# Spectral filter and token mixer, two layers: normalised rows of the inverse steps one step later in ScalarE's order, the doubled tile's low part inside those steps, and the last rows of the first layer written in four pieces

## Chip, cores and metric

One core of a Trainium2 chip runs the whole kernel. The metric is the device time of one execution in microseconds. The kernel before took 1017.25 us as the median of 3 runs (1016.85 to 1018.95).

## What is computed

x is 2048 tokens by 640 channels, f32. A layer has two halves: a spectral filter over the layer-normalised x (2-D FFT, a product with complex weights, inverse FFT), and a token mixer, an MLP over the tokens. Each is added to x. Two layers follow each other with the same weights.

```python
def _A_ref(x, w_r, w_i):
    X = jnp.fft.rfft2(x, axes=(-2, -1))
    X = X * (w_r + 1j * w_i)
    return jnp.fft.irfft2(X, s=(S, D), axes=(-2, -1))

def _B_ref(x, w1, b1, w2, b2):
    h = _layernorm(x, axis=-1)
    u = jnp.einsum("bsd,sf->bdf", h, w1) + b1      # w1: 2048 x 1728
    u = _gelu(u)
    y = jnp.einsum("bdf,fs->bds", u, w2) + b2      # w2: 1728 x 2048
    return y.transpose(0, 2, 1)

x = x + _A_ref(_layernorm(x), A_w_r, A_w_i)
x = x + _B_ref(_layernorm(x), B_w1, B_b1, B_w2, B_b2)
x = x + _A_ref(_layernorm(x), A_w_r, A_w_i)
x = x + _B_ref(_layernorm(x), B_w1, B_b1, B_w2, B_b2)
```

## The kernel before

x lies in 16 row tiles of 128 tokens by 640 channels, numbered 0 to 15 (`NJ` = 16). Products that need more than half precision are made from pairs of f16 tiles: a high part (`...h`) and a low part (`...l`), the difference from the f32 value. A full product is three matmuls (high by high, low by high, high by low).

**Stages.** The first layer runs: the filter's forward stages (to about 130 us of the profile), its inverse steps (method `a2`, to about 184 us), the mixer's first product with W1 (`b1st`, to about 376 us), its second product with W2, row by row (still `b1st`, to about 562 us), and a tail that joins it to the filter's first stage of the second layer. The second layer has the same inverse steps (about 640 to 693 us) and a mixer of its own form (`b2nd`, to the end). 

**Inverse steps** (`a2`). Step i of NJ + 5 works on several rows at once, each in another phase: on row i the matmuls of one inverse stage and ScalarE's `eh`; on row i-1 VectorE's `el` and the matmuls of the other inverse stage; on row i-2 the additions to `xt` on VectorE and GpSimd, and the store; on row i-3 the layer norm's statistics on VectorE (`st`, `mv`, `v`); on row i-4 the scale `r` and offset `nb` on GpSimd (`r` by a power), and then `hf`, the normalised row, on ScalarE, for some rows with a f16 copy (`hha`, `hh`). The tiles `xt` have five buffers, and the load of row i+1 is issued in step i. The steps run in program order on every engine (`self.pin`, which makes the helper at line 59 keep each instruction's place), so an instruction that waits holds all that stands behind it on its engine. All compute instructions carry line 59, the helper's; they are told apart by their tiles.

**The doubled tile.** One weight tile of W1 has 64 columns left; its other half holds the low part of the same columns. `wsplit` writes it in two chunks: ScalarE the high columns into `wh` and a copy into `wl` (steps 12 and 13 of `a2`), VectorE the rest, `wh<-raw,s,wl`, two instructions of 128x512, at the start of `b1st` and of `b2nd`. In `b1st` the 16 subtractions `hl = hf - hh` follow on VectorE.

**Rows of the second product** (`b1st`). For each row j, 28 groups (14 tiles of the hidden width, two halves of 320 channels) of three matmuls, two for the short tile: 82. Then VectorE adds the PSUM tile to `xt` (`xt<-ps,c,xt`), which frees it, and the row is prepared for the next layer's filter: statistics (VectorE), `r` and `nb` (GpSimd), `z` (ScalarE), `eo` (first fold, GpSimd), `f` (second fold, VectorE), `fh` (ScalarE), `fl` (VectorE). s1, the filter's first stage, is 15 small matmuls `tM,fh`/`tM,fl` into a PSUM tile, and `s1h` (ScalarE) and `s1l` (VectorE) take it over. `pend` holds rows that wait for s1; `flush(k)` issues s1 until k rows are left. After row j `flush(1)` issues s1(j-2). The next rows' weight tiles are made on the way: `wh` on ScalarE, `wl` on VectorE. Until row 15 no order is pinned here and the scheduler sorts. Row 15 runs its two halves one after the other, in program order; between them, `flush(0)` issues s1(13), and the second fold and `fh` of row 14 are written. After the second half, `a0_tail` makes `fl` and s1 of row 14 and, in two parts (`ft`, `fht`, `flt`), all of row 15. The next stage (`tD,s1h`, `tD,s1l`) needs all 16 rows.

Of the kernel before, what the change touches and what calls it, by code (L numbers as in the profile page):

```python
# [10 lines left out]
F32 = mybir.dt.float32  # L11
# [3 lines left out]
AF = mybir.ActivationFunctionType  # L15
# [4 lines left out]
S, D, NL, F = 2048, 640, 321, 1728  # L20
NJ, NG, NFT = 16, 16, 14
# [13 lines left out]
HA = range(8)  # L35
# [31 lines left out]
class Layers:  # L67
# [644 lines left out]
    def a2(self, li):  # L712
        nc, A = self.nc, self.A
        first = li == 0
        V, G, T = self.V, self.G, self.T
# [9 lines left out]
        p = self.push("a2", side=self.sq)  # L725

        xts = [p.tile([128, 642], F32, name=f"xt{i}_{self.n}") for i in range(5)]
# [10 lines left out]
        def xload(j):  # L738
            nc.sync.dma_start(xts[j % 5][:, :D], self.xs[li][j])
            return xts[j % 5]  # L740
# [36 lines left out]
        xt, pd, eo, p1, ec, mv, vs, rb = ({} for _ in range(8))  # L777
# [3 lines left out]
        for i in range(NJ + 5):  # L781
            has = [0 <= i - k < NJ for k in range(6)]
            if has[0]:
                pd[i] = id_mm(i)
            if has[1]:
                k = i - 1
                eh, ps = eo[k], pd.pop(k)
                el = elow(ps, eh)
                if not first and i == NJ:
                    self.pss0 = self.big()  # L790
                    for j in HA:
                        for a in range(2):
                            mm(self.pss0[:, a, :320], self.w[0][0][:, j], self.hh[j][:, a], start=j == 0, stop=False)
                p1[k] = is1_mm(eo.pop(k), el, tIM[k // 4][:, k % 4])
            if first and i == 10:
                next(sc)
            if has[4]:
                v, mean = vs.pop(i - 4)
                r = self.t(p, [128, 1], F32, "r", 2)
                G.tensor_tensor(r, v, self.mh, op=ALU.pow)  # L800
                b = self.t(p, [128, 1], F32, "nb", 2)
                G.tensor_scalar(b, mean, r, -1.0, op0=ALU.mult, op1=ALU.mult)
                rb[i - 4] = r, b
            if has[2]:
                k = i - 2
                x, ps = xt[k], p1.pop(k)
                o = ps[:, 1]
                e = self.t(p, [128, 324], F32, "ec", 2)
                T.activation(e[:, :322], ps[:, 0, :322], AF.Copy)
                V.tensor_tensor(v2(x, 160, NL), v2(x, 160, NL), v2(o, 161, 1), op=ALU.subtract)  # L810
                V.tensor_tensor(x[:, :NL], x[:, :NL], o[:, :NL], op=ALU.add)
                if first and i == 11:
                    next(sc)
                G.tensor_tensor(v2(x, 160, NL), v2(x, 160, NL), v2(e, 161, 1), op=ALU.add)
                G.tensor_tensor(x[:, :NL], x[:, :NL], e[:, :NL], op=ALU.add)
            if has[4]:
                r, b = rb.pop(i - 4)
                f = self.hf[i - 4]
                T.activation(f, xt.pop(i - 4)[:, :D].rearrange("p (a b) -> p a b", a=2), AF.Identity, scale=r, bias=b)
                if i - 4 in HA:  # L820
                    T.activation(self.hh[i - 4], f, AF.Copy)
            if 1 <= i and i + 1 < NJ:
                xt[i + 1] = xload(i + 1)
            if has[2]:
                nc.sync.dma_start(self.xs[li + 1][i - 2], xt[i - 2][:, :D])
            if has[3]:
                st = self.stats1(p, xt[i - 3])
                m = self.stats2(p, st)
                v = self.t(p, [128, 1], F32, "v", 2)
                V.tensor_scalar(v, m[:, 1:2], (1.0 + EPS) / ZS ** 2, EPS * EPS / ZS ** 2, op0=ALU.mult, op1=ALU.add)  # L830
                vs[i - 3] = v, m[:, 0:1]
            if has[0]:
                eo[i] = ehigh(pd[i])
            if i == 3:
                self.wload(1)
                self.wopen(1)
            if first:
                if i in (6, 7):
                    self.scan1(1, (i - 6,))
                if i == 8:  # L840
                    sc = self.scale1(1, at=lambda: p1[i - 1][:, 1, 400:401])
                    next(sc)
            if i in (12, 13):
                self.wsplit(1, (i - 12,), lo=False)
            if i in (1, 4, 8):
                mload()
        self.pin = False
# [81 lines left out]
    def b1st(self, li):  # L929
        nc, A = self.nc, self.A  # L930
        V, G, T = self.V, self.G, self.T
# [5 lines left out]
                T.activation(self.hh[j], self.hf[j], AF.Copy)  # L937
        sc = {m: self.scale1(m) for m in range(2, NFT + NJ)}
        self.pin = True
        self.wsplit(1, hi=False)  # L940
        self.wload(2)
        self.scan1(2)
        self.h = []
# [13 lines left out]
        p = self.pz = self.push("b1", side=self.sq)  # L957
# [50 lines left out]
        for ft in range(NFT):  # L1008
# [10 lines left out]
            for j in run:  # L1019
# [20 lines left out]
                else:  # L1040
# [16 lines left out]
                    if ft >= NFT - 2 and 1 < j < 14 and j % 2 != ft % 2:  # L1057
                        i = SEQ[(j - 2) // 2 + 6 * (ft - NFT + 2)]
                        usplit(i, uf[i])
            dup, i = ft == 1, SEQ[ft]  # L1060
# [26 lines left out]
        p = self.pT  # L1087
# [10 lines left out]
        xts = [load(0), load(1)]  # L1098
        pend = []

        def flush(k):
            while len(pend) > k:
                self.s1_all(*pend.pop(0))

        for j in range(NJ):
            wh, wl = self.w.pop(NFT + j)
            ahead(NFT + j, (wh, wl))
            m = NFT + j
            steps = prep(m)
            c2 = self.ct[1][:, j:j + 1]  # L1110
            if j + 2 < NJ:
                xts.append(load(j + 2))
            xt = xts[j][:, :D]
            T.activation(xt, xt, AF.Identity, bias=self.b2[:, j:j + 1])
            x2 = xt.rearrange("p (a b) -> p a b", a=2)
            tail = j == NJ - 1
            ps = self.big()
            pss = (ps[:, 0], self.big()[:, 0] if tail else ps[:, 1])
            order = [(ft, a) for ft in SEQ for a in range(2)]
            if tail:  # L1120

                order.sort(key=lambda q: q[1])
                st = self.t(p, [128, 2, 6], F32, "st", 2)
                self.pin = True

            def half(a):
                V.scalar_tensor_tensor(x2[:, a], pss[a][:, :320], c2, x2[:, a], op0=ALU.mult, op1=ALU.add)
                V.bn_stats(st[:, a], x2[:, a])

            for i, (ft, a) in enumerate(order):  # L1130
                if tail and i == NFT:
                    half(0)
                    flush(0)
                    pend.append((j - 1, *self.a0_hi(self.a0_fold2(late))))
                if i in (4, 8):
                    next(steps, None)
                if i in (6, 7):
                    step(m + 2)
                if i in (15, 18):
                    self.scan1(m + 3, (i // 3 - 5,))  # L1140
                if i == 26 and m + 3 < NFT + NJ:
                    step(m + 3)
                o = pss[a][:, :320]
                if ft < NFT - 1:
                    self.mm3(o, (wh[:, ft], wl[:, ft]), (uh[ft][:, a], ul[ft][:, a]), ft == SEQ[0], ft == SEQ[-1])
                else:
                    mm(o, wh[:, ft], ul[ft][:, a], start=False, stop=False)
                    mm(o, wl[:, ft], uh[ft][:, a], start=False, stop=False)
            if tail:
                half(1)  # L1150
                nc.sync.dma_start(self.xs[li + 1][j], xt)
                self.a0_tail(j, xts[j], st, pend)
                self.pin = False
                break
            V.scalar_tensor_tensor(x2, ps[:, :, :320], c2, x2, op0=ALU.mult, op1=ALU.add)
            nc.sync.dma_start(self.xs[li + 1][j], xt)
            flush(1)
            r, b = self.stats_r(p, *self.stats(p, xt, self.CA, self.CB))
            late = self.a0_fold1(self.a0_norm(xt, r, b))
            if j < NJ - 2:  # L1160
                pend.append((j, *self.a0_lo(*self.a0_hi(self.a0_fold2(late)))))
        self.pop("a0")
        self.pop("u")
        self.pop("wr2")
# [14 lines left out]
    def b2nd(self, li):  # L1179
# [6 lines left out]
        V, T, G = self.V, self.T, self.G  # L1186
# [220 lines left out]
        first, last = (collections.defaultdict(list) for _ in range(2))  # L1407
        lam = lambda f, *a: lambda: f(*a)
        A2, A4 = slice(0, 2), slice(2, 4)
        for d in range(ND):  # L1410
            i = {a: at[d, a] for a in PB}
# [17 lines left out]
        self.pin = True  # L1429
        fetch(0)  # L1430
        fetch(1)
        self.wsplit(1, hi=False)
        pr = self.push("br", side=self.sp)
        (wh0, wl0), (wh1, _) = self.w.pop(0), self.w.pop(1)
        pss = self.pss0, self.big()
        early, late, low, high = range(NJ - 4), range(NJ - 4, NJ), range(8), range(8, NJ)
# [23 lines left out]
        p = self.push("b1", side=self.sq)  # L1460
# [94 lines left out]
        def xload(d):  # L1555
            if d < NQ:
                xts[d] = self.t(p, [128, 2, 2, 320], F32, "xt", 3)
                for i in range(2):
                    nc.sync.dma_start(row(d, i), self.xs[li][E[d] + NQ * i])
# [402 lines left out]
```

## Time and profile before

| | us |
|---|---|
| median of 3 runs | 1017.25 (1016.85 to 1018.95) |
| profiled execution | 1017.07 |
| its span, first to last instruction | 1015.3 |
| mean granted TensorE clock | 0.979 of full |

| engine | busy us |
|---|---|
| TensorE (PE) | 969.4 |
| VectorE (DVE) | 781.8 |
| ScalarE (ACT) | 576.5 |
| GpSimd (POOL) | 300.0 |

A row of a timeline gives the start, the time that the merged instructions cover (us), the engine, the line, the operation, the tiles (out<-in) with their shapes, how many instructions are merged, and in brackets the idle time of the engine before them with what ended it. Buffer numbers are left out, so `xt` is any row. Busy times of neighbours overlap a little, as each instruction's own latency is counted in; an engine's pace is read from the starts. In a row of waits stand the waiting engine and tile, the releaser, the total in us, how many waits, and the longest. In the table by stretches each engine has its busy time and, in brackets, its instructions; the three last numbers are the granted clock, the DMA engines' busy share and GB/s.

### The profile page before, as it was taken

How to read it: one execution, taken by the hardware profiler on the slowest of the kernel's cores; microseconds unless marked ns; L12 is line 12 of the kernel's file. 1: busy time of each engine (PE TensorE's matmuls, PEld its weight loads, DVE VectorE, ACT ScalarE, POOL GpSimd, SP SyncE). 2: the span in 40 equal slices, each digit the busy share in tenths (PEclk: the TensorE clock that was granted, in tenths of full speed). 3: DMA queues.
4: the chain of work that ended last, by engine and by line, in shares of the span. 5: the costliest groups of instructions: out<-in, count | busy, mean ns of one | idle time of the engine just before them, and what ended most of it. 6: DMA issues, size and time to landing. Idle time of an engine off the chain costs nothing.

```text
span 1015.3 us, 20992 instructions
## 1 busy us (share of the span) xinstructions
PE 969.4 (95%) x8235; PEld 721.2 (71%) x8235; DVE 781.8 (77%) x1493; ACT 576.5 (57%) x890; POOL 300.0 (30%) x502
## 2 busy tenths in 40 slices
PE   4889999999999999999999799999999999999998
PEld 3778777677777667777777688776777777677776
DVE  7978978988777784666666689789965557998885
ACT  5857668687666455555553377685643454544531
POOL 6937857412212201222222277574000000000000
PEclk9599999999999999999999999999999999999999
DMA  7865356557657546464423455365444446755411
GB/s 232 279 185 164 115 178 219 206 187 255 236 195 250 186 124 246 139 193 146 126 89 117 126 181 181 105 229 204 159 156 164 145 142 228 245 177 190 153 45 53
DMA packets 67259, 176.45 MB, mean 174 GB/s; under 512 B 7996, under 2 KB 15320, under 8 KB 67160
## 3 DMA queue, kind: packets, MB, share of 16 engines
q1 hardware_dynamic: 59384, 146.92, 45.1%
q0 software_dynamic: 7776, 28.20, 7.5%
q8 instruction: 64, 1.05, 0.4%
q14 instruction: 35, 0.29, 0.1%
HBM read 127.24 MB, written 47.84 MB: 172 GB/s over the span
## 4 chain that ended last, share of the span: by engine, by line
PE 36%; DVE 13%; ACT 6%; POOL 3%; issue 3%; DMA 2%; SPq 0%; ACTq 0%; DVEq 0%; POOLq 0%
PE ps L59 36%; DVE wl L59 3%; DMA xt<-x 2%; DVE st L59 2%; DVE xt L59 1%; POOL eo L59 1%; DVE f L59 1%; ACT wh L59 1%; ACT xt L59 1%; ACT z L59 1%; DVE s1l L59 1%; ACT junk L59 1%; POOL xt L59 1%; DVE Yl L59 1%; DVE S L59 1%
## 5 line engine op out<-in xcount | busy, mean ns | idle before, releaser
L59 PEld LDWEIGHTS <-wh 128*128 128x128 f16 x2602 | 251.9, 98 | 103.6 <-issue 5.0
L59 PEld LDWEIGHTS <-wl 128*128 128x128 f16 x1610 | 157.5, 98 | 66.0 <-DVE wl L59 2.8
L59 PE MATMUL ps<-ul,wh 128*128 128x320 f16 x448 | 133.9, 301 | 0.6 <-DVE ul L59 0.6
L59 PE MATMUL ps<-uh,wl 128*128 128x320 f16 x448 | 133.9, 301 | 0.1
L59 PE MATMUL ps<-uh,wh 128*128 128x320 f16 x416 | 124.8, 300 | 1.6 <-DVE s L59 1.6
L59 PE MATMUL ps<-hl,wh 128*128 128x320 f16 x496 | 102.2, 299 | 0.9 <-DVE hl L59 0.9
L59 PEld LDWEIGHTS <-wo 128*128 128x128 f16 x756 | 73.9, 98 | 29.4 <-DVE wo L59 0.8
L59 DVE SCALAR_TENSOR_TENSOR wl<-raw,s,wh 128x896 f16<-128x896 f32 (+2 forms) x64 | 75.0, 1176 | 12.9 <-ACT wh L59 12.7
L59 ACT ACTIVATE junk<-raw 128x896 bf16<-128x896 f32 (+1 forms) x60 | 59.5, 991 | 44.2 <-DMA raw<-w 44.0
L59 POOL TENSOR_TENSOR r<-v,mh 128x1 f32<-128x1 f32 x64 | 36.4, 569 | 158.4 <-DVE nm L59 149.0
L59 PE MATMUL ps<-tDi,Yh 128*128 128x322 f16 x320 | 71.3, 300 | 0.2
L59 DVE TENSOR_TENSOR f<-eo 128x256 f32<-128x256 f32 (+1 forms) x124 | 39.1, 368 | 40.7 <-POOL eo L59 40.1
L59 ACT ACTIVATE wh<-raw,s 128x896 f16<-128x896 f32 (+2 forms) x68 | 67.2, 1010 | 2.3 <-DVE s L59 1.6
L59 POOL TENSOR_TENSOR xt<-xt,ec 128x320 f32<-128x320 f32 x64 | 52.5, 842 | 34.2 <-DVE xt L59 34.0
L59 ACT ACTIVATE z<-xt,nb,r 128x640 f32<-128x640 f32 x31 | 28.5, 919 | 57.6 <-POOL z L59 45.3
L59 PE MATMUL ps<-ph,tS 128*128 128x321 f16 (+2 forms) x288 | 58.5, 286 | 1.3 <-DVE tb L59 1.3
L59 PE MATMUL ps<-u,wo 128*128 128x320 f16 x420 | 59.0, 299 | 0.5 <-DVE wo L59 0.5
L59 DVE BATCH_NORM_STATS2 st<-xt 128x6 f32<-128x320 f32 x126 | 55.3, 480 | 5.2 <-DMA xt<-x 4.5
L59 PE MATMUL ps<-hha,wh 128*128 128x320 f16 x288 | 58.1, 299 | 0.9 <-DVE wh L59 0.9
L59 POOL TENSOR_TENSOR eo<-z 128x320 f32<-128x320 f32 x62 | 53.3, 881 | 17.0 <-ACT z L59 15.1
L59 PE MATMUL ps<-tM,f 128*128 128x128 f32 x160 | 39.5, 426 | 19.6 <-DVE f L59 19.6
L59 PE MATMUL ps<-tDi,Yl 128*128 128x322 f16 x192 | 55.7, 299 | 1.7 <-DVE Yl L59 1.7
(251 smaller groups left out, 2376.6 us busy)
## 6 DMA issues: line engine op xcount, KB each, us to landing
xt<-x SPq DMA_DIRECT2D x79, 320.0 KB
raw<-w SPq DMA_DIRECT2D x32, 512.0 KB
w<-w SPq DMA_DIRECT2D x48, 321.0 KB
x<-xt SPq DMA_DIRECT2D x47, 320.0 KB
raw<-w SPq DMA_DIRECT2D x32, 448.0 KB
raw<-w2z SPq DMA_DIRECT2D x32, 448.0 KB
w1S<-sp POOLq DMA_DIRECT2D x20, 512.0 KB, 3.7
out<-xt SPq DMA_DIRECT2D x15, 320.0 KB
```

The lines of the kernel that those rows point to most:

```text
L59: i = f(*a, **k)
```

## The change

Four edits. In `a2`, `hf` (and its copy) of row i-5 stands in step i in place of that of row i-4; step 16 does two rows, and the steps after it do row i-4 again. `r` and `nb` get a third buffer. The load of row i is issued in step i, not that of row i+1. The two VectorE instructions of the doubled tile move from the start of `b1st` and of `b2nd` into steps 14 and 15 of `a2`. In `b1st`, rows 13 and 14 are prepared by a generator `last` in four pieces, which the next row's loop draws at its groups 6, 12 and 17 (the first piece is drawn at once); half of the first fold moves from GpSimd to VectorE there; the order is pinned from the end of row 13 on; the bias of rows 14 and 15 is added together; and s1 is issued inside the loops: s1(11) and s1(12) at group 2 of row 14, s1(13) at group 2 and s1(14) at group 22 of row 15.

```diff
--- before.py
+++ after.py
@@ -796,9 +796,9 @@
                 next(sc)
             if has[4]:
                 v, mean = vs.pop(i - 4)
-                r = self.t(p, [128, 1], F32, "r", 2)
+                r = self.t(p, [128, 1], F32, "r", 3)
                 G.tensor_tensor(r, v, self.mh, op=ALU.pow)
-                b = self.t(p, [128, 1], F32, "nb", 2)
+                b = self.t(p, [128, 1], F32, "nb", 3)
                 G.tensor_scalar(b, mean, r, -1.0, op0=ALU.mult, op1=ALU.mult)
                 rb[i - 4] = r, b
             if has[2]:
@@ -813,14 +813,16 @@
                     next(sc)
                 G.tensor_tensor(v2(x, 160, NL), v2(x, 160, NL), v2(e, 161, 1), op=ALU.add)
                 G.tensor_tensor(x[:, :NL], x[:, :NL], e[:, :NL], op=ALU.add)
-            if has[4]:
-                r, b = rb.pop(i - 4)
-                f = self.hf[i - 4]
-                T.activation(f, xt.pop(i - 4)[:, :D].rearrange("p (a b) -> p a b", a=2), AF.Identity, scale=r, bias=b)
-                if i - 4 in HA:
-                    T.activation(self.hh[i - 4], f, AF.Copy)
-            if 1 <= i and i + 1 < NJ:
-                xt[i + 1] = xload(i + 1)
+            for k in (i - 5,) if i < NJ else (i - 5, i - 4) if i == NJ else (i - 4,):
+                if not 0 <= k < NJ:
+                    continue
+                r, b = rb.pop(k)
+                f = self.hf[k]
+                T.activation(f, xt.pop(k)[:, :D].rearrange("p (a b) -> p a b", a=2), AF.Identity, scale=r, bias=b)
+                if k in HA:
+                    T.activation(self.hh[k], f, AF.Copy)
+            if 2 <= i < NJ:
+                xt[i] = xload(i)
             if has[2]:
                 nc.sync.dma_start(self.xs[li + 1][i - 2], xt[i - 2][:, :D])
             if has[3]:
@@ -842,6 +844,8 @@
                     next(sc)
             if i in (12, 13):
                 self.wsplit(1, (i - 12,), lo=False)
+            if i in (14, 15):
+                self.wsplit(1, (i - 14,), hi=False)
             if i in (1, 4, 8):
                 mload()
         self.pin = False
@@ -937,7 +941,6 @@
                 T.activation(self.hh[j], self.hf[j], AF.Copy)
         sc = {m: self.scale1(m) for m in range(2, NFT + NJ)}
         self.pin = True
-        self.wsplit(1, hi=False)
         self.wload(2)
         self.scan1(2)
         self.h = []
@@ -1102,6 +1105,17 @@
             while len(pend) > k:
                 self.s1_all(*pend.pop(0))
 
+        def last(j, xt):
+
+            rb = self.stats_r(p, *self.stats(p, xt, self.CA, self.CB))
+            yield
+            eo = self.a0_fold1(self.a0_norm(xt, *rb), sv=True)
+            yield
+            f = self.a0_hi(self.a0_fold2(eo))
+            yield
+            pend.append((j, *self.a0_lo(*f)))
+            yield
+
         for j in range(NJ):
             wh, wl = self.w.pop(NFT + j)
             ahead(NFT + j, (wh, wl))
@@ -1111,7 +1125,9 @@
             if j + 2 < NJ:
                 xts.append(load(j + 2))
             xt = xts[j][:, :D]
-            T.activation(xt, xt, AF.Identity, bias=self.b2[:, j:j + 1])
+            for k in {NJ - 2: (j, j + 1), NJ - 1: ()}.get(j, (j,)):
+                xk = xts[k][:, :D]
+                T.activation(xk, xk, AF.Identity, bias=self.b2[:, k:k + 1])
             x2 = xt.rearrange("p (a b) -> p a b", a=2)
             tail = j == NJ - 1
             ps = self.big()
@@ -1121,7 +1137,6 @@
 
                 order.sort(key=lambda q: q[1])
                 st = self.t(p, [128, 2, 6], F32, "st", 2)
-                self.pin = True
 
             def half(a):
                 V.scalar_tensor_tensor(x2[:, a], pss[a][:, :320], c2, x2[:, a], op0=ALU.mult, op1=ALU.add)
@@ -1130,8 +1145,12 @@
             for i, (ft, a) in enumerate(order):
                 if tail and i == NFT:
                     half(0)
+                if j == NJ - 2 and i == 2:
                     flush(0)
-                    pend.append((j - 1, *self.a0_hi(self.a0_fold2(late))))
+                if j >= NJ - 2 and i in (6, 12, 17):
+                    next(row)
+                if tail and i in (2, 22):
+                    flush(0)
                 if i in (4, 8):
                     next(steps, None)
                 if i in (6, 7):
@@ -1152,13 +1171,16 @@
                 self.a0_tail(j, xts[j], st, pend)
                 self.pin = False
                 break
+            self.pin = j >= NJ - 3
             V.scalar_tensor_tensor(x2, ps[:, :, :320], c2, x2, op0=ALU.mult, op1=ALU.add)
             nc.sync.dma_start(self.xs[li + 1][j], xt)
+            if self.pin:
+                row = last(j, xt)
+                next(row)
+                continue
             flush(1)
             r, b = self.stats_r(p, *self.stats(p, xt, self.CA, self.CB))
-            late = self.a0_fold1(self.a0_norm(xt, r, b))
-            if j < NJ - 2:
-                pend.append((j, *self.a0_lo(*self.a0_hi(self.a0_fold2(late)))))
+            pend.append((j, *self.a0_lo(*self.a0_hi(self.a0_fold2(self.a0_fold1(self.a0_norm(xt, r, b)))))))
         self.pop("a0")
         self.pop("u")
         self.pop("wr2")
@@ -1429,7 +1451,6 @@
         self.pin = True
         fetch(0)
         fetch(1)
-        self.wsplit(1, hi=False)
         pr = self.push("br", side=self.sp)
         (wh0, wl0), (wh1, _) = self.w.pop(0), self.w.pop(1)
         pss = self.pss0, self.big()
```

How the order changes, first on ScalarE in the inverse steps of the first layer. `hf_367_2430` to `2432` are the normalised rows 4 to 6, `eh` and `ec` belong to the rows ahead. Before:

```order
L59 ACTIVATE ec_2823<-ps_2762 128x322
L59 ACTIVATE hf_367_2430<-xt_368_2449,nb_2821,r_2819 128x640
L59 ACTIVATE hha_867<-hf_367_2430 128x640
L59 ACTIVATE eh_2840<-ps_2793,cxe 128x644
L59 ACTIVATE ec_2876<-ps_2812 128x322
L59 ACTIVATE hf_367_2431<-xt_368_2445,nb_2874,r_2872 128x640
```

Now:

```order
L59 ACTIVATE ec_2873<-ps_2809 128x322
L59 ACTIVATE hf_367_2430<-xt_368_2449,nb_2818,r_2816 128x640
L59 ACTIVATE hha_867<-hf_367_2430 128x640
L59 ACTIVATE eh_2890<-ps_2843,cxe 128x644
L59 ACTIVATE ec_2923<-ps_2862 128x322
L59 ACTIVATE hf_367_2431<-xt_368_2445,nb_2871,r_2869 128x640
```

`hf` of row 4 stood behind `ec_2823` (of the PSUM tile 2762) and now stands behind the one of the tile 2809, a step later. Of the `nb` it reads, the number is smaller than that of the `ec` before it by 2 then, and by 55 now: it is written a step before.

Second, VectorE around the end of row 13 of the first layer. `fl_7450` is the low part of row 12, `xt_7136<-ps_7458` takes row 13 from its PSUM tile, `s1l_5365` is the second half of an s1, `wl` the low part of row 15's weights. Before:

```order
L59 TENSOR_TENSOR fl_7450<-f_7442,fh_7448 128x640
L59 SCALAR_TENSOR_TENSOR xt_7136<-ps_7458,c_75,xt_7136 128x640
L59 SCALAR_TENSOR_TENSOR wl_7607<-raw_7291,s_73,wh_7606 128x896
L59 BN_STATS st_7574<-xt_7136 128x6 x2
L59 SCALAR_TENSOR_TENSOR s1l_5365<-ps_7556,s1h_5364 128x80x8
L59 BN_AGGR mv_7577<-st_7574 128x2
L59 SCALAR_TENSOR_TENSOR wl_7607<-raw_7293,s_73,wh_7606 128x896
```

Now:

```order
L59 TENSOR_TENSOR fl_7450<-f_7442,fh_7448 128x640
L59 SCALAR_TENSOR_TENSOR xt_7136<-ps_7458,c_75,xt_7136 128x640
L59 BN_STATS st_7556<-xt_7136 128x6 x2
L59 BN_AGGR mv_7559<-st_7556 128x2
L59 TENSOR_SCALAR v_7561<-mv_7559 128x1
L59 TENSOR_SCALAR nm_7563<-mv_7559 128x1
L59 SCALAR_TENSOR_TENSOR s1l_5365<-ps_7582,s1h_5364 128x80x8
L59 SCALAR_TENSOR_TENSOR s1l_5365<-ps_7600,s1h_5364 128x80x8
L59 SCALAR_TENSOR_TENSOR wl_7572<-raw_7291,s_73,wh_7571 128x896
```

The two `wl` of row 15 moved behind the statistics of row 13 and behind two `s1l`; `fl` of row 12 and the emptying of row 13 kept their places.

Third, PE inside row 14. `ps_7575` is row 14's PSUM tile now, `ps_7609` before; `ps_7600` is that of s1(12) now, `ps_7698` before; `fh_7448` is the high part of row 12. Before, the end of row 14 and the start of s1(12):

```order
L59 LDWEIGHTS wl_7453
L59 MATMUL ps_7609<-uh_546_3346,wl_7453 128x320
L59 LDWEIGHTS fh_7448
L59 MATMUL ps_7698<-tM_751_5375,fh_7448 128x128
L59 LDWEIGHTS fh_7448
```

Now, the end of s1(11), which stands behind six matmuls of row 14, and s1(12):

```order
L59 LDWEIGHTS fl_7289
L59 MATMUL ps_7582<-tM_751_5374,fl_7289 128x128
L59 LDWEIGHTS fh_7448
L59 MATMUL ps_7600<-tM_751_5375,fh_7448 128x128
L59 LDWEIGHTS fh_7448
L59 MATMUL ps_7600<-tM_751_5375,fh_7448 128x128
L59 LDWEIGHTS fl_7450
```

s1(12) moved from behind all 82 matmuls of row 14 to behind the first six of them and s1(11).

## The prediction

> **What bounds the kernel now.** I read the page's busy shares first, then a table by stretches, then the chain of waits, and only then single instructions at the three places that the change touches. The page:
>
> ```profile
> PE 969.4 (95%) x8235; PEld 721.2 (71%) x8235; DVE 781.8 (77%) x1493; ACT 576.5 (57%) x890; POOL 300.0 (30%) x502
> PE   4889999999999999999999799999999999999998
> ```
>
> TensorE is busy 95% of the span, so a change can gain only where PE stands still; the second row shows one dip in the middle, at about 560 us. The table by stretches (length, then busy time of PE, PEld, DVE, ACT, POOL, then PEclk):
>
> ```profile
> 155.00:184.00 29.00, 27.49 (x190) 20.34 (x189) 25.65 (x69) 23.99 (x39) 22.10 (x37) 1.00 0.64 204
> 184.00:203.00 19.00, 17.91 (x128) 12.38 (x128) 18.25 (x37) 10.49 (x16) 6.67 (x10) 1.00 0.62 215
> 640.00:672.00 32.00, 31.62 (x226) 24.14 (x227) 23.00 (x56) 20.15 (x31) 19.93 (x33) 1.00 0.55 172
> 672.00:693.00 21.00, 20.69 (x144) 15.68 (x143) 19.26 (x48) 17.77 (x30) 15.87 (x27) 1.00 0.70 236
> 693.00:700.00 7.00, 5.64 (x39) 3.62 (x38) 5.42 (x15) 5.35 (x9) 5.25 (x9) 1.00 0.43 159
> 562.00:567.00 5.00, 0.46 (x4) 0.11 (x2) 4.53 (x18) 1.10 (x2) 1.50 (x3) 1.00 0.17 66
> 567.00:571.00 4.00, 3.15 (x28) 2.90 (x28) 2.50 (x5) 1.67 (x4) 0.00 (x0) 0.57 0.30 82
> ```
>
> PE stands 1.51 us in 155 to 184 and 1.09 us in 184 to 203 (the end of the first layer's inverse steps and the products behind it), 0.38 + 0.31 + 1.36 us in 640 to 700 (the same in the second layer), and 4.5 us in 562 to 567, the tail of the first layer's rows. The tail is the only large hole, and behind it the granted clock is 0.57. The chain of waits puts the same places on the path:
>
> ```profile
> 382.22 8.62 DMA xt<-x
> ...
> 526.72 28.77 PE ps L59 x229
> ...
> 562.12 1.04 DVE f L59 x4
> ...
> 567.80 2.86 PE ps L59 x25
> ...
> 698.94 145.80 PE ps L59 x1072
> ```
>
> From 526.72 PE runs unbroken for 28.77 us through rows 13 and 14; before it, from 382.22, the chain goes through the loads and the rows' chain on VectorE, ScalarE and GpSimd. So at row 13 that chain is as long as PE's own work.
>
> **The change, part A: inverse steps of the first layer.** ScalarE's `hf` waits for GpSimd's `nb`, and that is handed on to `eh`, `el` and PE. First two rows: who waited for whom in 135 to 182; then PE's own waits in 150 to 184, and in 182 to 204:
>
> ```profile
> DVE el L59 <- ACT eh L59: 8.0, 8, 2.6
> ACT hf L59 <- POOL nb L59: 5.8, 6, 1.2
> ...
> PE ps L59 <- ACT eh L59: 0.8, 1, 0.8
> PE ps L59 <- DVE el L59: 0.7, 2, 0.5
> ...
> PE ps L59 <- DVE hl L59: 0.9, 4, 0.3
> ```
>
> With `hf` one step later, `nb` has been written a step before. The same instructions run, none is added. At best the stalls of 0.8 + 0.7 = 1.5 us go. The doubled tile's low part, two VectorE instructions, stood between the last statistics and the 16 `hl` subtractions, whose end sets PE:
>
> ```profile
> 188.42 0.89 DVE L59 BATCH_NORM_STATS2 st<-xt 128x6 f32<-128x320 f32 x2 [0.49 <-POOL xt L59]
> 189.65 1.40 DVE L59 SCALAR_TENSOR_TENSOR wh<-raw,s,wl 128x512 f16<-128x512 f32 x2
> 190.97 5.96 DVE L59 TENSOR_TENSOR hl<-hf,hha 128x640 f16<-128x640 f32 x8
> ...
> 202.94 0.84 PE L59 MATMUL ps<-hl,wh 128*128 128x320 f16 x5 [0.17 <-DVE hl L59]
> ```
>
> They take 190.97 - 189.65 = 1.3 us of that chain. They now stand in steps 14 and 15, where VectorE is busy 25.65 of 29 us: a step of 3.1 us has about 0.3 us free, and each gets 0.7. The work is moved into a stretch with little room, so the gain is not 1.5 + 1.3. PE's idle time in 155 to 203, 1.51 + 1.09 = 2.6 us, is the most; 0.8 is the least that I expect (1.3 less a push of some 0.5 on the last `el`). I take **-1.8 us**. The loads of x come one step later, with two steps (6 us) of lead; the first row's load in the chain above took 8.62 us when several were queued, so they are the risk of this part: should they be late, each would hold a step of PE.
>
> **Part B: the same in the second layer.** There the low part is waited for openly:
>
> ```profile
> 698.94 1.26 PE L59 MATMUL ps<-hha,wh 128*128 128x320 f16 x8 [0.89 <-DVE wh L59]
> ...
> 698.14 1.40 DVE L59 SCALAR_TENSOR_TENSOR wh<-raw,s,wl 128x512 f16<-128x512 f32 x2
> 688.68 0.92 ACT L59 ACTIVATE hf<-xt,nb,r 128x640 f32<-128x640 f32 x1 [1.35 <-POOL nb L59]
> ```
>
> The wait of 0.89 us goes, and of the other idle time there, 0.38 + 0.31 + 0.47, some 0.4. I take **-1.3 us** (-0.9 to -2.0). The chain above runs on PE for 145.80 us from 698.94, so nothing behind can give it back at once.
>
> **Part C: rows 13 to 15 of the first layer.** This decides the sign. In these rows `tM,fh`/`tM,fl` is the first stage s1 of an earlier row, 15 small matmuls; `fl` is its input, `xt<-ps,c,xt` empties a row's PSUM tile. VectorE, then PE:
>
> ```profile
> 532.40 0.83 DVE L59 TENSOR_TENSOR fl<-f,fh 128x640 f16<-128x640 f32 x1 [0.80 <-ACT fh L59]
> ...
> 543.68 0.83 DVE L59 TENSOR_TENSOR fl<-f,fh 128x640 f16<-128x640 f32 x1 [0.80 <-ACT fh L59]
> 544.42 0.88 DVE L59 SCALAR_TENSOR_TENSOR xt<-ps,c,xt 128x640 f32<-128x640 f32 x1
> ...
> 563.27 0.54 DVE L59 SCALAR_TENSOR_TENSOR zt<-ps,c,zt 128x320 f32<-128x320 f32 x1
> ...
> 566.93 0.82 DVE L59 TENSOR_TENSOR fl<-f,fh 128x640 f16<-128x640 f32 x1
> ...
> 536.93 0.28 PE L59 MATMUL ps<-tM,fh 128*128 128x128 f16 x2
> ...
> 537.76 0.30 PE L59 MATMUL ps<-uh,wh 128*128 128x320 f16 x1
> ...
> 548.90 0.28 PE L59 MATMUL ps<-tM,fh 128*128 128x128 f16 x2
> ...
> 561.88 0.30 PE L59 MATMUL ps<-uh,wl 128*128 128x320 f16 x1
> 564.18 0.28 PE L59 MATMUL ps<-tM,fh 128*128 128x128 f16 x2 [2.01 <-ACT fh L59]
> 567.80 0.29 PE L59 MATMUL ps<-tM,fl 128*128 128x128 f16 x1 [3.33 <-DVE fl L59]
> ...
> 572.07 0.24 PE L59 MATMUL ps<-tD,s1l 128*128 128x160 f16 x1 [0.41 <-DVE s1l L59]
> ```
>
> PE ends row 13 at 536.93, but VectorE empties that row only at 544.42: it is 7.5 us behind. Before, that cost nothing, since s1(12) stood behind all 82 matmuls of row 14, at 548.90, and its `fl` (543.68) was there. Now s1(12) stands behind six of them and s1(11). Six at (548.90 - 537.76) / 82 = 0.136 us and one s1 of 0.83 (536.93 to 537.76) bring PE there at 538.6. `fl` of row 12 is ready at 544.5, and the PSUM tile, the one of row 13, at 545.3. PE stands **6.7 us** (5.9 if only `fl` counts). Behind it wait the other 76 matmuls of row 14, all of row 15, and everything later on PE; VectorE's next `s1l` too, ahead of row 15's `wl`.
>
> From 545.3: s1(12) 0.8, 76 x 0.136 = 10.3, row 15 82 x 0.136 = 11.2, s1(13) and s1(14), which now also stands inside row 15, 1.7: 569.3. A hole of this kind was followed by a granted clock of 0.57 (562 to 571 above); the 1.6 us or so that I let run at half speed cost 0.8, so the row ends at 570.1. The last half is taken up by VectorE at 570.2, against 563.27: +6.9.
>
> The tail is shorter, which is this part's gain. From 563.27 to 572.07 it took 8.8 us, with `fl` of row 14 (0.7) and its s1 on PE (567.80 to about 569.2, 1.4 at half clock) inside; both are gone from it, but PE's group then waits for the scaled low parts that follow. Between 0.7 (only `fl`) and 2.0 I take 1.3. **C = 6.9 - 1.3 = +5.6 us** (+4.1 with the shorter stall and the larger tail gain, +7.1 with 0.9 more at half clock and the smaller one).
>
> The addition of rows 13 and 14 that moves from GpSimd to VectorE is hidden: both wait for `z` there.
>
> By the Trainium skill (TensorE: Matmul & The Clock Gate, Part 1, the HAM clock gate) the array falls to half clock after an idle window of about 3.4 us and comes back after a busy one; the 0.57 behind the 4.5 us hole agrees. By that rule a full window at half speed could follow the new stall, an estimate of 1.7 us in place of my 0.8, and the sum would be 0.9 higher.
>
> **Sum.** -1.8 - 1.3 + 5.6 = +2.5 us. The profiled execution took 1017.07 us (span 1015.3 and 1.8 around it), 0.18 below the median of 1017.25, inside the runs' spread. 1017.07 + 2.5 = **1019.6 us**. From the bounds of all parts, the likeliest case reaches from 1016.6 (-2.6 - 2.0 + 4.1 = -0.5) to 1022.5 (-0.8 - 0.9 + 7.1 = +5.4).
>
> **The rivals.**
>
> *The rows' chain is in time.* If VectorE were not behind PE at row 13, s1(12) would run at once. Then C is: s1(14) inside row 15, +0.8; the last half no longer behind the fold of row 14 (563.27 against PE's end at 562.0), -1.1; the tail -1.3: -1.6, and the sum -4.7, 1012.4 us. For it: the chain gains on PE (543.68 - 532.40 = 11.3 us a row, against 548.90 - 536.93 = 12.0), and its start is set by a load. Against it: it would have to gain 7 us, and nothing in the change touches rows 0 to 12. 0.15.
>
> *A and B bring nothing.* The steps' real limit may be VectorE, which gets 0.7 us more in steps 14 and 15, or the loads of x with their shorter lead. Then C stands alone: 1017.07 + 5.6 = 1022.7 us, and 1 us more if the last `el` is pushed beyond what `hl` gains. For it: 25.65 of 29 us busy. Against it: the waits for `nb`, 5.8 us, and the open wait of 0.89. 0.25.
>
> *A shorter stall.* If another buffer is given to s1(12), and the chain, tied to the earlier end of A through PE, has gained on row 13, the stall could be some 4 us and the clock stay up: C = +2.6, sum -0.5, 1016.6 us, no change. 0.13.
>
> **How the numbers follow.** Forecast 0.47, the rivals 0.15, 0.25, 0.13. About 0.2% (2 us) is what can be told from no change here. Of the forecast's 0.47, 0.27 lies above 1019.3, 0.17 within, 0.03 below; with the second rival whole, slower is 0.52. The third rival gives 0.09 to the same and 0.04 to faster: same 0.26, and faster 0.15 + 0.03 + 0.04 = 0.22. The range reaches up to the second rival and down half way to the first: 1014 to 1023; the likeliest case's own is 1016.6 to 1022.5.
>
> **What would show it.** In the profile after: a PE wait of 5 to 7 us for `fl` or for the emptying of a row, after six matmuls of row 14, as a second dip of PE near 540 us; a clock below 1 just behind it; no wait of `hf` for `nb` and no wait for the low part at the second layer's first product; from the last half to the second stage 7 to 8 us in place of 8.8. It is wrong if PE passes row 14 without standing, or if PE's idle time in the inverse steps grows.

## The result, and the profile after

The change made the kernel slower: 1021.37 us as the median of 8 runs (1019.60 to 1024.43), against 1018.32 for the kernel before in the 8 runs beside it (1016.50 to 1019.31). The ratio is 1.0035, with a 95% interval of 1.0022 to 1.0049.

The page's first two rows after:

```profile
PE 973.9 (95%) x8235; PEld 724.4 (71%) x8235; DVE 784.0 (77%) x1495; ACT 579.0 (57%) x890; POOL 302.2 (30%) x500
PE   4899999999999999999997799999999999999998
```

The ratio stands for 3.6 us; the two medians are 3.05 apart. TensorE does the same 8235 matmuls; the dip in the middle has become two slices wide. The table by stretches, at the places shown before and at the new hole (length, busy time of PE, PEld, DVE, ACT, POOL, then PEclk):

```profile
155.00:184.00 29.00, 28.99 (x204) 22.18 (x204) 27.95 (x75) 26.53 (x42) 23.60 (x38) 1.00 0.73 241
693.00:700.00 7.00, 6.66 (x46) 4.85 (x45) 6.86 (x17) 5.44 (x9) 5.79 (x9) 1.00 0.90 301
...
537.00:541.00 4.00, 0.00 (x0) 0.00 (x0) 1.25 (x6) 0.94 (x2) 1.81 (x3) 0.97 0.08 29
541.00:547.00 6.00, 4.92 (x27) 3.31 (x28) 5.30 (x10) 4.08 (x6) 1.10 (x4) 0.50 0.15 57
569.00:572.00 3.00, 0.00 (x0) 0.00 (x0) 2.71 (x9) 0.00 (x0) 1.41 (x2) 0.91 0.28 109
572.00:581.00 9.00, 6.79 (x50) 5.95 (x51) 3.14 (x9) 2.37 (x6) 0.00 (x0) 0.50 0.61 196
```

In the first layer's inverse steps PE no longer stands (28.99 of 29 us). From 537 to 541 it does nothing at all, and the 6 us behind it run at half clock; the tail's hole, too, is followed by 9 us at half clock. PE's own timeline in row 14, the tail, and then VectorE at the same places:

```profile
536.58 0.22 PE L59 MATMUL ps<-tM,fl 128*128 128x128 f16 x1
541.62 0.40 PE L59 MATMUL ps<-tM,fh 128*128 128x128 f16 x2 [4.82 <-ACT fh L59]
542.48 0.29 PE L59 MATMUL ps<-tM,fl 128*128 128x128 f16 x1 [0.46 <-DVE fl L59]
...
573.17 0.39 PE L59 MATMUL ps<-tM,fht 128*128 128x128 f16 x2 [4.20 <-ACT fht L59]
...
576.62 0.31 PE L59 MATMUL ps<-tD,s1l 128*128 128x160 f16 x1 [0.28 <-DVE s1l L59]
...
541.60 0.82 DVE L59 TENSOR_TENSOR fl<-f,fh 128x640 f16<-128x640 f32 x1 [0.80 <-ACT fh L59]
542.34 0.88 DVE L59 SCALAR_TENSOR_TENSOR xt<-ps,c,xt 128x640 f32<-128x640 f32 x1
...
569.01 0.55 DVE L59 SCALAR_TENSOR_TENSOR zt<-ps,c,zt 128x320 f32<-128x320 f32 x1 [0.89 <-PE ps L59]
```

s1(11) ends at 536.8; s1(12) waits 4.82 us for `fh` of row 12 and 0.46 for its `fl`, 5.3 in all. Its `fl` stands where it stood before, just ahead of the emptying of row 13. The tail takes 576.62 - 569.01 = 7.6 us, against 8.8.

In the second layer the wait for the doubled tile is gone, and another has come:

```profile
710.40 0.43 PE L59 MATMUL ps<-hhb,wh 128*128 128x320 f16 x2 [1.17 <-ACT hhb L59]
...
708.66 0.92 ACT L59 ACTIVATE hf<-xt,nb,r 128x640 f32<-128x640 f32 x1 [3.01 <-POOL nb L59]
...
704.46 1.72 POOL L59 TENSOR_TENSOR r<-v,mh 128x1 f32<-128x1 f32 x1 [0.53 <-DVE v L59]
706.28 2.35 POOL L59 TENSOR_SCALAR nb<-mv,r 128x1 f32<-128x1 f32 x1
...
704.29 5.69 DVE L59 TENSOR_TENSOR hl<-hf,hha 128x1280 f16<-128x1280 f32 x4
```

`r` and `nb` of the last row, one column each, take 1.72 and 2.35 us on GpSimd, while VectorE runs `hl` from 704.29 on. Row 14's `r` just ahead took 0.55. The same two operations in the kernel before, where VectorE ran the doubled tile's low part from 698.14 and `hl` from 699.47:

```profile
698.38 0.92 POOL L59 TENSOR_TENSOR r<-v,mh 128x1 f32<-128x1 f32 x1 [0.60 <-DVE v L59]
699.39 1.61 POOL L59 TENSOR_SCALAR nb<-mv,r 128x1 f32<-128x1 f32 x1
```

A table of stretches between the same matmuls in every kernel's profile makes the parts comparable (us, differences of PE starts). A: from the first `el,tIM` to the 32nd `hl,wh` of the first layer. W1: on to the first matmul of row 0. Rows: on to the first `tD,s1l` behind the tail; "13 on" is the part of it from the first matmul of row 13. Next: on to the last `ph,tS` of the second layer's filter. B: on to the last `hhb,wl`. Behind B all take 170.6.

| kernel | A | W1 | rows | 13 on | next | B |
|---|---|---|---|---|---|---|
| before | 66.97 | 163.95 | 205.18 | 46.52 | 61.31 | 207.79 |
| after | 64.72 | 164.55 | 210.85 | 53.01 | 63.70 | 208.22 |
| no_rows | 64.70 | 163.77 | 205.01 | 46.50 | 63.58 | 208.19 |
| hf_only | 64.97 | 164.74 | 205.12 | 46.48 | 61.31 | 206.97 |
| split_only | 67.01 | 164.43 | 204.41 | 46.48 | 61.31 | 209.42 |
| rows_only | 66.93 | 161.99 | 209.00 | 52.13 | 63.27 | 207.74 |
| late_s1 | 64.69 | 162.12 | 208.61 | 50.05 | 62.51 | 208.21 |
| late_s1_split1 | 64.70 | 162.07 | 206.17 | 49.25 | 63.87 | 207.02 |
| late2 | 64.71 | 164.27 | 204.06 | 46.56 | 63.93 | 208.19 |
| late2_warm | 64.71 | 162.31 | 203.90 | 45.09 | 61.47 | 208.19 |
| late2_hold | 64.71 | 162.89 | 203.32 | 46.53 | 63.02 | 206.97 |
| late2_both | 64.71 | 162.58 | 203.31 | 46.54 | 63.12 | 206.87 |
| late2_more | 64.72 | 164.71 | 203.20 | 46.02 | 61.83 | 206.86 |

A and B repeat within 0.3 us wherever the code there is the same. W1 does not: 162.0 to 164.7 in kernels that are equal there, so 2 us of a single profile say nothing. The same holds for rows 0 to 12, whose code is the same in every kernel and which take 156.8 to 158.8 ("rows" less "13 on"); "13 on" is 46.5 in all four kernels with the old last rows, so what the rows' edits do is read there: +6.5 in the change. The profiled execution of the change took 1024.43 us, the longest of its 8. Of the 7.4 us by which its span is longer (1022.7 against 1015.3), A gives -2.25, rows +5.67, next +2.39, B +0.43, W1 +0.60, and 0.54 arises ahead of A.

### The profile page after: what moved, and what is told of

The parts are those of the page before. It is cut to its first block, busy times and chain, and to the rows that moved or that the text cites. A ratio compares the mean times of both kernels' runs of the same rounds, so it can differ in the third digit from the quotient of the medians.

```text
span 1022.7 us, 21015 instructions
## 1 busy us (share of the span) xinstructions
PE 973.9 (95%) x8235; PEld 724.4 (71%) x8235; DVE 784.0 (77%) x1495; ACT 579.0 (57%) x890; POOL 302.2 (30%) x500
## 4 chain that ended last, share of the span: by engine, by line
PE 39%; DVE 11%; ACT 5%; DMA 4%; POOL 3%; issue 2%; SPq 0%; ACTq 0%; DVEq 0%; POOLq 0%
PE ps L59 39%; DMA xt<-x 3%; DVE wl L59 3%; POOL eo L59 1%; DVE st L59 1%; ACT z L59 1%; ACT wh L59 1%; DVE f L59 1%; DVE xt L59 1%; DVE s1l L59 1%; ACT junk L59 1%; ACT xt L59 1%; DMA raw<-w2z 1%; DVE S L59 1%; DVE Yl L59 1%
## 5 line engine op out<-in xcount | busy, mean ns | idle before, releaser
L59 POOL TENSOR_TENSOR r<-v,mh 128x1 f32<-128x1 f32 x64 | 39.0, 609 | 158.9 <-DVE nm L59 149.2
```

The source lines that it names most:

```text
L59: i = f(*a, **k)
```

## The experiments

Each ratio is against runs of the kernel before on the same chip, with its 95% interval. Three chips were used: one for no_rows, rows_only, late_s1 and late_s1_split1, one for the four kernels from late2 to late2_both, one for hf_only, split_only and late2_more. Differences between ratios of different groups are across chips.

**no_rows: the edits of the inverse steps alone.** The part of the diff in the rows' loop of `b1st` is taken back.

> The inverse steps' edits alone (hf one step later, the doubled tile's low part in steps 14 and 15), the last rows as before. Theory: the first layer's steps gain 1.7 us, the second layer's gain of 0.9 is given back by a new wait of 1.2 us for the last normalised row (GpSimd's last r and nb are slow while VectorE runs hl), so 1 to 2 us faster than before, with no PE wait near 540 us. Rival (these edits bring nothing): the time of before, within 0.5 us.

0.9985 (0.9968 to 1.0002), medians 1015.39 against 1017.10. The size is the theory's, and the interval just reaches no change. The trace has the two halves apart: A -2.27, B +0.40. PE's waits in 640 to 720:

```profile
PE ps L59 <- ACT hhb L59: 2.1, 4, 1.2
PE ps L59 <- DVE Yl L59: 0.8, 1, 0.8
```

The longest wait for `hhb`, 1.2 us, is the one of the change, with rows as before; it belongs to the inverse steps' edits.

**rows_only: the edits of the last rows alone.**

> The last rows' edits alone, the inverse steps as before. Theory: PE stands 5 to 6 us for row 12's low part in row 14, with half clock behind it, 4 to 6 us slower than before, and slower than the whole change by the 1 to 2 us that the inverse steps gain. Rival (the inverse steps' edits cost and the rows pay for it): faster than the whole change.

1.0048 (1.0032 to 1.0064), +4.9 us by the ratio (medians 1023.12 against 1017.10, of 6 runs). The rows' edits alone are slower than before and no_rows is not, so the rival, that the inverse steps cost and the rows pay, is out. That the rows alone cost more than the whole change is likely, not shown: the two intervals overlap. The two ratios add up: 1.0048 and 0.9985 to 1.0033, against 1.0035.

**late_s1: s1(12) fourteen groups of matmuls later.**

```diff
                 if j == NJ - 2 and i == 2:
-                    flush(0)
+                    flush(1)
+                if j == NJ - 2 and i == 16:
+                    flush(0)
```

> The whole change, but in row 14 only s1(11) stands at group 2, and s1(12) at group 16. Theory: no PE wait in row 14 and no half clock there, so 5 to 7 us less than the whole change, 2 to 4 us less than before; the idle time in the tail (4.5 us) and the half clock behind it stay. Rival (the rows' chain sets the end anyway, the wait moves to row 15): within 2 us of the whole change.

1.0020 (1.0009 to 1.0031): 1.5 us below the change's ratio, not 5 to 7, with intervals that overlap, and still above before. The rival was nearer. In the profiles the rows from 13 on take 50.05, against 53.01 in the change and 46.52 before. PE's waits in 530 to 575 of this kernel:

```profile
PE ps L59 <- ACT fht L59: 4.2, 1, 4.2
PE ps L59 <- DVE fl L59: 1.9, 1, 1.9
PE ps L59 <- ACT fh L59: 1.6, 1, 1.6
```

Row 14 no longer stands, but s1(13), at group 2 of row 15, now waits 1.6 + 1.9 = 3.5 us for its `fh` and `fl`, and behind that 3.4 us run at half clock (550.0 to 553.4). The wait moved a row on, since the rows' chain stays as far behind PE as it was.

**late_s1_split1: the same, with the doubled tile's low part at the start of the second layer's product again.**

```diff
-            if i in (14, 15):
+            if first and i in (14, 15):
                 self.wsplit(1, (i - 14,), hi=False)
...
         fetch(1)
+        self.wsplit(1, hi=False)
```

> As late_s1, but the doubled tile's low part stands at the start of the second layer's product again (the first layer keeps it in the steps). Theory: the second layer then waits 0.9 us for the low part and less than 0.3 us for the last normalised row, in place of 1.2 us: within 0.5 us of late_s1. Rival (the move gains its 0.9 us there): 0.9 to 1.3 us slower than late_s1.

1.0005 (0.9990 to 1.0020), 1.5 us below late_s1 with intervals that overlap. The trace decides against the rival, that taking the move back costs 0.9 to 1.3: B falls by 1.19 us (208.21 to 207.02). The theory was also wrong in one number: the wait for `hhb` did not go, it is 1.4 us at the longest.

**late2: every s1 placed behind its own row's chain.** s1(12) at group 16 of row 14, s1(13) at group 16 of row 15, s1(14) behind row 15.

```diff
                 if j == NJ - 2 and i == 2:
-                    flush(0)
+                    flush(1)
+                if j >= NJ - 2 and i == 16:
+                    flush(0)
...
-                if tail and i in (2, 22):
-                    flush(0)
...
         for k, f, fh in pend:
-            ps.append((k, self.a0_s1(k, *self.a0_lo(f, fh))))
+            ps.append((k, self.a0_s1(k, f, fh)))
```

> The whole change, with s1(12) at group 16 of row 14, s1(13) at group 16 of row 15, and s1(14) behind row 15 (its second half s1l in the tail). Theory (the rows' chain is 7 us behind PE, so each s1 must stand that much later): no PE wait from row 13 to the end of row 15, 3 to 5 us less than late_s1, 1.5 to 3 us less than before. Rival (the tail's length sets the time, whatever stands in the rows): within 1 us of late_s1.

0.9982 (0.9969 to 0.9996), medians 1015.91 against 1017.68: 1.8 us less than before and 3.8 less than late_s1 by the ratios. In the trace there is no wait in rows 13 to 15; those left are in the tail, the longest these:

```profile
PE ps L59 <- ACT fht L59: 3.1, 1, 3.1
PE ps L59 <- DVE fl L59: 1.9, 1, 1.9
```

So the cost of the rows' edits was the place of the s1, not the writing in pieces. The rows are 1.1 us shorter than before in the profile, but all of that lies in rows 0 to 12, where the code is the same; from row 13 on they take 46.56 against 46.52. late2 and no_rows also have nearly one ratio (0.9982 and 0.9985), so the pieces show no gain.

**late2_warm: matmuls that nobody reads, in the tail's idle time.**

```diff
         ps = []
+        dummy = self.big()[:, 0, :320]
+        for k in range(24):
+            self.PE.matmul(dummy, keep[0][:, 0], keep[1][:, 0], start=True, stop=True)
         for k, f, fh in pend:
...
```

`keep` holds two tiles that the last row leaves, `wh` and `uh`.

> As late2, with 24 further matmuls of 128x320 in the tail, where PE has nothing to do; nobody reads their result. Theory (the half clock behind the idle tail costs time in the next stage): the granted clock stays at 1 behind the tail, 1.5 to 3 us less than late2. Rival (the next stage is not bound by the clock, or the matmuls delay the tail): 0 to 1 us more than late2.

0.9972 (0.9960 to 0.9984). The stretch behind the tail, first of late2, then of late2_warm:

```profile
565.50:575.70 10.20, 7.90 (x59) 7.07 (x60) 4.46 (x12) 3.25 (x7) 0.00 (x0) 0.50 0.54 182
```

```profile
562.00:572.00 10.00, 6.61 (x81) 5.44 (x78) 5.93 (x15) 3.96 (x8) 0.27 (x1) 1.00 0.58 193
```

late2 runs 10.2 us at half clock there, late2_warm none, and the stretch "next" is 61.47 in place of 63.93. By the ratios the gain is 1.0 us, less than the 1.5 to 3 expected, with intervals that overlap.

**late2_hold: VectorE waits for the last `nb`.**

```diff
                 rb[i - 4] = r, b
+                if not first and i - 4 == NJ - 1:
+                    hold = self.t(p, [128, 1], F32, "hold", 1)
+                    V.tensor_copy(hold, b)
```

> As late2, with one copy of 128x1 on VectorE at the end of the second layer's inverse steps that reads the last nb, so that hl starts only when GpSimd is done. Theory (hl on VectorE slows the two last operations on GpSimd): r and nb of the last row take 0.6 and 0.3 us in place of 1.7 and 2.4, the PE wait of 1.2 us for the last normalised row goes, about 1 us less than late2. Rival (GpSimd is slow there for a reason of its own, or hl is then late for PE): no change or slower.

0.9968 (0.9956 to 0.9981). GpSimd, then VectorE, of this kernel:

```profile
694.36 0.55 POOL L59 TENSOR_TENSOR r<-v,mh 128x1 f32<-128x1 f32 x1 [0.54 <-DVE v L59]
695.00 0.27 POOL L59 TENSOR_SCALAR nb<-mv,r 128x1 f32<-128x1 f32 x1
...
695.30 0.15 DVE L59 COPY hold<-nb 128x1 f32<-128x1 f32 x1 [1.03 <-POOL nb L59]
695.37 5.69 DVE L59 TENSOR_TENSOR hl<-hf,hha 128x1280 f16<-128x1280 f32 x4
```

With VectorE idle for 1.03 us, `r` and `nb` take 0.55 and 0.27, as the theory said, `hl` is not late for PE, and B is 1.22 us shorter than in late2 (206.97 against 208.19). By the ratios the gain is 1.4 us, a little more than B explains, with intervals that overlap; the trace is what shows the cause.

**late2_both** has both additions.

> late2 with both additions. Theory: both gains, 2.5 to 4 us less than late2, 4 to 6 us less than before.

0.9961 (0.9946 to 0.9976): 4.0 us less than before and 2.1 less than late2, at or a little below the low end of what was expected. In its profile 6.8 us from the end of the tail on still ran at half clock ("next" 63.12), so the 24 matmuls do not always keep the clock.

**hf_only and split_only: the two edits of the inverse steps one by one.** The first keeps the lines on `hf`, `r`, `nb` and the loads, the second those on `wsplit`.

> Only hf one step later (with the third buffer and the later loads of x), in both layers. Theory: the PE stalls of 1.5 us in the first layer's steps go, but the 16 hl still stand behind the doubled tile, so the first layer gains 0.5 to 1 us and the second 0.3: 0.8 to 1.3 us less than before. Rival (all of the gain of no_rows comes from this edit): 1.5 to 2 us less.

> Only the doubled tile's low part in steps 14 and 15, in both layers. Theory: without the room that the later hf makes, VectorE's added 0.7 us a step delays the last el, and what hl gains (1.3 us) is given back in part; in the second layer the new wait for the last normalised row takes the 0.9: 0 to 0.8 us less than before. Rival: 1.5 to 2 us less.

hf_only: 0.9981 (0.9968 to 0.9993), 1.9 us less than before, the rival's size, though the interval takes in the theory's as well. split_only: 1.0022 (1.0009 to 1.0035), 2.2 us more, outside both expectations. PE's waits in 135 to 205 of split_only, then in 640 to 720 of split_only and of hf_only:

```profile
PE ps L59 <- DVE el L59: 1.0, 3, 0.5
PE ps L59 <- DVE hl L59: 0.7, 3, 0.3
PE ps L59 <- ACT eh L59: 0.6, 1, 0.6
...
PE ps L59 <- ACT hhb L59: 2.3, 2, 2.1
```

```profile
PE ps L59 <- ACT hhb L59: 1.6, 2, 1.4
```

In the first layer the later `hf` alone gives A -2.00, which is the rival's reading and not the theory's 0.5 to 1, and the moved low part alone +0.04; both give -2.27. In the second layer the later `hf` alone gives B -0.82 and the moved low part alone +1.63, with a wait of 2.1 us for the last normalised row.

**late2_more: 14 further unread matmuls,** between s1(14) and row 15's own s1.

> late2_both with 14 more unread matmuls between s1(14) and row 15's own s1. Theory: the last 2.2 us of idle time there go and with them the half clock in the next stage: 0.5 to 2 us less than late2_both. Rival (the matmuls delay the tail by their own time): 0 to 1 us more.

0.9954 (0.9939 to 0.9969), medians 1012.70 against 1017.74. It is the fastest version, 4.7 us less than before. Behind the tail:

```profile
562.00:572.00 10.00, 8.22 (x93) 6.49 (x92) 6.70 (x19) 2.81 (x6) 1.41 (x2) 1.00 0.45 158
```

No half clock is left there. Against late2_both the difference is 0.7 us, within the intervals and on another chip.

## Why the prediction was right, point by point

The forecast was +2.5 us, the measurement is 1.0035, +3.6 us of 1018.32 (2.2 to 5.0); the sign and the place of the loss were right, three terms were not what they seemed. That the sum came as near as it did is in part luck: A and B together brought 1.5 us by no_rows in place of 3.1, and C cost 4.9 by rows_only in place of 5.6, two errors of opposite effect.

**A was right in size (-1.8; the trace has -2.25) and half wrong in reason.** The stalls on `nb` went, as row 155 to 184 shows. Of the 1.3 us that the moved low part was to take off the chain to `hl` little came: split_only gains nothing there, and hf_only has 2.00 of the 2.27, so 0.27 is left for it (hf_only's trace has no wait for `hl`, but one of 1.7 us for `hh`, which the change has not). "The work is moved into a stretch with little room" was true to that point.

**B was wrong: -1.3 forecast, +0.4 measured.** The later `hf` alone brought 0.82 (hf_only); the moved low part took it back. The step that failed is "The wait of 0.89 us goes ... so nothing behind can give it back at once". The wait went, but the low part had kept VectorE from `hl` while GpSimd made the last `r` and `nb`; with `hl` at once, these took 4.1 us in place of 2.5 (0.92 + 1.61 in the trace of before), and PE waited 1.17 us for the last normalised row. late2_hold shows it: with VectorE held, 0.8 us, and B 1.2 us shorter.

**C was right: +5.6 forecast; from row 13 on the change takes 6.5 us longer in the profile, rows_only 5.6, and rows_only costs 4.9 by its runs.** Its terms were off in opposite ways, and that they nearly cancel is luck too. The stall is 5.3 us, not 6.7: PE took s1(12) up at 541.62, ahead of the emptying of row 13 at 542.34, by which the 6.7 were reckoned, so s1(12) did not need that row's PSUM tile; it waited for `fh` and `fl` alone. The half clock behind it cost more than 0.8: from 541.62 to 547 PE ran at 0.50, 4.9 us of matmuls, so some 2.5, an estimate. The tail is 7.6 us in place of 8.8, -1.2 against -1.3. With the forecast's own +0.8 for s1(14) and -1.1 for the fold these make 6.3 of the 6.5 us. By the Trainium skill (TensorE: Matmul & The Clock Gate, Part 1, the HAM clock gate) a busy window of about 3.4 us is needed before the clock comes back. The trace agrees: the 6 us at 0.50 follow the 4 idle us, PE is busy without a break from 544.1 to 547.5, and behind that the clock is full.

**A term was missing.** The tail's idle time is followed by half clock in the next stage, 9 us of it in the profile of the change, which made that stretch 2.4 us longer than before. no_rows has it as well (63.58) with the old tail, so it can come without the rows' edits, and before, hf_only and split_only have not (61.31). Whether the edits of the rows make it likelier stays open: all six profiles with them and without the unread matmuls have 62.5 to 63.9, but there is only one profile of each kernel.

**The rivals.** That the rows' chain is in time is out: PE waited where forecast. "A and B bring nothing" was half true: B brought nothing, A did (-2.25 in the profile). The shorter stall came (5.3 in place of 6.7), and s1(12) had another buffer as that rival supposed, but the clock did not stay up.

## What to carry to other kernels

Ask of every consumer that is issued earlier whether its producer's chain is on time at the new place: here PE was 7.5 us ahead of VectorE and stood for most of it, and moving one consumer only moved the wait to the next row until each had been placed behind its own chain. A small operation on a slow helper engine can be covered by work that looks like the thing to remove; look at what else ran during a wait before removing it. Idle time of TensorE should be counted with the half clock behind it, and filling the last hole with matmuls that nobody reads was worth trying, though its gain of about 1 us lies within the intervals.

## What was not expected of the hardware

GpSimd's operations of one column depend on what VectorE runs beside them: `r` took 0.55 us and `nb` 0.27 with VectorE idle (late2_hold), 0.92 and 1.61 with the doubled tile's low part and then `hl` (before), 1.72 and 2.35 with `hl` alone (after). It is not any work of VectorE: row 14's `r` and `nb` took 0.55 and 0.27 beside `st`, which reads one tile. By the Trainium skill (SBUF — State Buffer, the section on its two separate sides) the two engines share a pair of ports as an exclusive lock: whichever instruction starts first holds it for its whole length, a VectorE instruction with two SBUF inputs among them. The traces agree: `hl` has two such inputs, and one of its four instructions takes 5.69 / 4 = 1.4 us. In the traces of before, after, hf_only and split_only the last row's `r` ends 0.41 us, and its `nb` 0.05 us, after the end of such an instruction of VectorE; that is what a wait for the lock would look like. In the change `nb`, at 706.28 to 708.63, starts during the second `hl` and ends only behind the third (708.58), so it did not get in between the two.
